# Five block-product passes, a seeded second DFT and ScalarE statistics in an FNet layer with a gated feed-forward

## The chip, the core and the metric

The kernel runs on one core of one Trainium2 chip. The metric is the device time of one execution in microseconds (us); less is better. Times given for a version are medians of several executions; beside them stands one execution that the hardware profiler recorded. The engines are PE (TensorE, matrix products into PSUM), DVE (VectorE), ACT (ScalarE), POOL (GpSimd) and SP (SyncE, whose queue here issues the DMA transfers). Each engine works through its own list of instructions in order, and waits on semaphores for the others.

## The reference

The input x has 2048 rows (the sequence) of 448 columns. A Fourier layer and a gated feed-forward layer follow each other, each on a normalised input and with a residual.

```python
a = jnp.einsum("bsd,ed->bse", x, dft_hid_re)
b = jnp.einsum("bsd,ed->bse", x, dft_hid_im)
y = jnp.einsum("ts,bse->bte", dft_seq_re, a) - jnp.einsum("ts,bse->bte", dft_seq_im, b)
...
g = jnp.einsum("bsd,df->bsf", x, w_gate)
u = jnp.einsum("bsd,df->bsf", x, w_up)
h = _gelu(g) * u
return jnp.einsum("bsf,fd->bsd", h, w_down)
...
h = x + _A_ref(_layernorm(x, axis=-1), A_dft_seq_re, A_dft_seq_im, A_dft_hid_re, A_dft_hid_im)
h2 = h + _B_ref(_layernorm(h, axis=-1), B_w_gate, B_w_up, B_w_down)
```

## The kernel before, in words

Every product is made with operands split into two float16 parts (a high and a low part), three matmuls for one. ACT writes the high part (`hi_part`, L107), DVE the low part from the difference (`lo_part`, L110).

**The sequence DFT** comes first and runs in 64 steps (`N_STEPS`, loop at L816). The first 16 steps make two of the eight pairs of row blocks at once. From step 16 on, four steps are a pass: a pair p (2 to 7) and one of its two parts, real or imaginary. A plain step reads one tile of the DFT matrix (wr, loaded by `seq_load`), splits it into ws (`seq_hi`, `seq_lo`, three steps ahead of its use) and multiplies it with the normalised x (xs): 24 matmuls of 448 columns. The last three passes (steps from `FAST` = 52 on) are made by Strassen-like block products: seven products of half-size blocks in place of eight, 42 matmuls of 224 columns in a step. They need sums of blocks of the DFT matrix (`fast_sums` on DVE, then `fast_raw` and `fast_split` for the two tiles of a unit), sums of blocks of x (the tiles t, `t_load` to `t_lo`), and at the end of the pass the seven products are put together on DVE (`fast_out`, e). A unit is listed two steps ahead of its use; in the last step of a pass its parts stand between the parts of `fast_out`. Both kinds of pass write zs, from which `z_turn` makes z by transposing DMAs.

**The second DFT** (`hid_mm`, L708) multiplies z of a pair p, in two halves g of 128 rows, with the hidden DFT matrix wh: 21 matmuls of 448 columns into a PSUM bank y. It stands on PE between the two halves of the sequence steps m and m + 1, with m = 19, 24, 29, 36, 44, 52, 60 for p = 0 to 6; p = 7 comes within the next stage. DVE then adds x to it (`hid_add`, L722; the tile hx, loaded one step before), takes the statistics of h (`ffn_moments`) and `rstd` makes the factor of the second normalisation.

**The order** is written by hand: the tables `early` (work listed at the start of a step, behind the step's own splits) and `after` (behind its first or second half of matmuls) say at which step a piece of work stands. Each engine's list follows from the order of these calls. Buffers rotate: six ws tiles, five wr tiles, seven PSUM banks for the passes and one bank, tr, for y.

**The feed-forward** follows: 42 gate and up products in three blocks of rows (`GateUp`), then the down products. Its weights are split by `Weights`, ten chunks f during the DFT (`DFT_F`) and four during the first block (`JIT_F`), stored to w_dram and read back as gw; the last three of the DFT stay in their three tiles.

Of the kernel before, what the change touches and what calls it, by code (L numbers as in the profile page):

```python
# [21 lines left out]
NB = 4  # L22
# [10 lines left out]
def kernel(  # L33
# [92 lines left out]
    def root(mv, tag):  # L126
        n = mv.shape[1]
        sd = small.tile([P, n], F32, tag=f"sd{n}", name=f"sd_{tag}")
        A.activation(sd, mv[:, :, 1], AF.Sqrt, scale=1.0 / X_SC**2, bias=eps_t)
        return sd  # L130
# [5 lines left out]
    def rstd(mv, sd, tag, pool=small):  # L136
# [4 lines left out]
        V.tensor_scalar(r[:, 1], mv[:, :, 1], EPS, -0.5 / X_SC**2, op0=ALU.add, op1=ALU.mult)  # L141
# [26 lines left out]
    def pair_tile(name):  # L168
        return ring.tile([P, 2, D], F32, tag="xh", bufs=5, name=name)

    def w_tile(name):
        return ring.tile([P, 28 * P], F16, tag="w", bufs=3, name=name)
# [25 lines left out]
    def ffn_rstd(q, j):  # L198
        tag = f"h{q}_{j}"
        mv = moments[q, j]  # L200
        moments[q, j] = mv, rstd(mv, root(mv, tag), tag, const)

    def ffn_stats(q, j, h):
        for g in range(2):
            ffn_moments(q, j, h, g)
        ffn_rstd(q, j)
# [18 lines left out]
    def ffn_norm(q, j, h):  # L225
        tag = f"h{q}_{j}"
        mv, r = moments.pop((q, j))
        xn = fops.tile([P, 2, D], F32, tag="xn", name=f"xn_{tag}")
        for g in range(2):
            normed(xn[:, g, :], h[:, g, :], mv, r, g)  # L230
        ffn[q, j] = xn

    def ffn_bias(q, j):
        mv, r = moments[q, j]
        V.scalar_tensor_tensor(mv[:, :, 1], mv[:, :, 0], -1.0, r, op0=ALU.mult, op1=ALU.mult)
# [81 lines left out]
    class Weights:  # L317


        def __init__(self, f):  # L320
            self.f = f
# [26 lines left out]
        def hi(self, of_raw):  # L348
            if of_raw:
                self.w = w_tile(f"gu_w{self.f}")  # L350
            for s0, s1, src in self.parts(of_raw):
                hi_part(self.slots(0, s0, s1, src), src, W_SC)
# [100 lines left out]
    FAST = N_STEPS - 12  # L453
    A_RAW = ("A12", "A11", "A22")
    FORMS = ("S1", "S2", "S3", "S4")
# [11 lines left out]
    def fast_sums(n):  # L467
        fast_s[n] = dft.tile([P, 8 * P], F32, tag="wr", bufs=5, name=f"sums{n}")
        fast_w[n] = [fast_tile(n, k, **place) for k, place in enumerate(fast_places(n))]
        raw, s, src, dst = fast_views(n)  # L470
        V.tensor_add(s[:, 0], raw[:, :, 3], raw[:, :, 2])
        V.tensor_sub(s[:, 1], s[:, 0], raw[:, :, 1])
        V.tensor_sub(s[:, 2], raw[:, :, 1], raw[:, :, 3])
        V.tensor_sub(s[:, 3], raw[:, :, 0], s[:, 1])
# [54 lines left out]
    def fast_halves(n, g):  # L529
        p, part, qq = step_of(n)  # L530
        hi, lo = [zs[p][:, g, l, part * D : (part + 1) * D] for l in range(2)]
        src = fast_e[n][:, g * D : (g + 1) * D]
        hi_part(hi, src)
        lo_part(lo, src, hi)

    def fast_out(n, k):
# [10 lines left out]
        def plus(dst, m, src):  # L547
            V.scalar_tensor_tensor(c[dst], fast_sum(n, m), sc, c[src], op0=ALU.mult, op1=ALU.add)
# [37 lines left out]
    def t_tile(j):  # L586

        if j in (0, 1):
            if j == 0:
                fast_t["01"] = fops.tile([P, 8 * D], F16, tag="xs", name="t01")  # L590
            return fast_t["01"][:, j * 4 * D : (j + 1) * 4 * D]
# [4 lines left out]
        if j == 6:  # L596
            return ring.tile([P, 4 * D], F16, tag="xh", bufs=5, name="t6")
        if j == 7:
            return prep.tile([P, 4 * D], F16, tag="raw", bufs=2, name="t7")
        return fops.tile([P, 4 * D], F16, tag="xn" if j == 2 else "tt", name=f"t{j}")  # L600
# [101 lines left out]
    def h_tile(q, j):  # L702
        hp[q, j] = pair_tile(f"hx{q}_{j}")
# [26 lines left out]
    gu = {}  # L730
    DFT_F = ((13, 17), (12, 20), (11, 25), (9, 29), (7, 33), (5, 37), (3, 41), (0, 45), (1, 48), (2, 50))
    JIT_F = range(4, 11, 2)
# [10 lines left out]
    for f, n in DFT_F:  # L743
        at(after, (n - 4, 0), lambda f=f: gu.update({f: Weights(f)}))
# [5 lines left out]

    turns = [(16, 0), (20, 1), (25, 1), (32, 0), (40, 0), (48, 0), (57, 0)]
    for p, (n, half) in enumerate(turns):
        b, j = divmod(p, 2)
        m = (19, 24, 29, 36, 44, 52, 60)[p]
        at(early, m - 1, lambda b=b, j=j: h_tile(b, j))
        for g in range(2):

            at(after, (m + g, int(p == 6 and g)), lambda p=p, g=g: hid_mm(p, g), lambda p=p, g=g: hid_add(p, g))
        at(after, (n, half), lambda p=p: z_turn(p))
        at(early, m + 2 if p < 5 else N_STEPS - 7 + p, lambda b=b, j=j: ffn_stats(b, j, hp[b, j]))  # L760
        at(after, (m + 2, 0), lambda b=b, j=j: h_store(b, j))
        if b < 2:

            m += 2 if p == 3 else 0
            at(early, m + 2, lambda b=b, j=j: ffn_norm(b, j, hp[b, j]))
# [7 lines left out]
    for j, n in ((4, 28), (5, 31), (6, 39), (2, 43), (3, 45), (0, 47), (1, 49), (7, 53)):  # L773
# [139 lines left out]
    gu[JIT_F[0]] = Weights(JIT_F[0])  # L913
    z_turn(NP - 1)
    down_sums(0)
    gu[JIT_F[1]] = Weights(JIT_F[1])
# [7 lines left out]
    gw = {f: gu[f].w for f in range(3)}  # L924

# [101 lines left out]
    class GateUp:  # L1027
# [7 lines left out]
        def bank(self, k):  # L1035
            pool, tag = ps_gu, "XYZ"[k]
            if self.block == 0 and self.t % 2 == 0:
                pool, tag = ps_dn, f"a{k}"
            if self.block > 0 and k == 1 and self.t % 2 == 0:
                pool, tag = ps_tr, "tr"  # L1040
            return pool.tile([P, 512], F32, tag=tag, name=f"p{'XYZ'[k]}_{self.name}")[:, : self.n]
# [74 lines left out]
    def gw_load(t):  # L1116
        gw[t] = w_tile(f"gw{t}")
# [74 lines left out]
    def dn_banks(p):  # L1192

        if p == 6:
            places = [(ps_gu, "X"), (ps_tr, "tr"), (ps_gu, "Z"), (ps_gu, "Y")]
        else:
            places = [(ps_dn, f"a{k}") for k in range(4)]
        acc_d[p] = [pool.tile([P, 512], F32, tag=tag, name=f"acc_d{p}_{k}") for k, (pool, tag) in enumerate(places)]
# [22 lines left out]
    def hr_load(p):  # L1221
        hr[p] = pair_tile(f"hr{p}")
# [45 lines left out]
    ps_gu = ctx.enter_context(tc.tile_pool(name="ps_gu", bufs=1, space=bass.MemoryType.PSUM, reuse_waits="tile"))  # L1268
    ps_dn = ctx.enter_context(tc.tile_pool(name="ps_dn", bufs=1, space=bass.MemoryType.PSUM, reuse_waits="tile"))
# [9 lines left out]
    for t in range(NF):  # L1279
# [77 lines left out]
        if w and w.f + 4 in JIT_F:  # L1357
            gu[w.f + 4] = Weights(w.f + 4)
# [181 lines left out]
```

## Time and profile before

| what | us |
|---|---|
| median of 3 executions (lowest to highest) | 710.85 (710.21 to 710.87) |
| the profiled execution | 711.16 |
| its span, first to last instruction | 708.7 |
| DVE busy in the span | 531.7 |
| ACT busy in the span | 353.3 |
| POOL busy in the span | 92.6 |

The profile names each instruction by its line in the source; a matmul's row shows out<-in by the program's names. Three views are used below: the page (shares, slices and the chain of work that ended last), the same chain in order of time (a start, a duration, what ran), and the timeline of one engine (a start, a duration, line and operation, how many, and in brackets the idle time before it with what ended it). "x2" means two instructions in a row. A lookup of short stretches gives each engine's busy time, the count of its instructions in parentheses, and the granted clock of PE.

### The profile page before, as it was taken

To read this page: it belongs to the slowest core of one execution; us is meant where nothing else is said; L and a number is where in the kernel's file an instruction comes from. 1 tells how busy PE (TensorE), PEld (TensorE's weight loads), DVE (VectorE), ACT (ScalarE), POOL (GpSimd) and SP (SyncE) were. 2 spreads that over 40 slices of the span, in tenths; PEclk is the share of its full clock that TensorE was granted. 3 is DMA by queue.
4 is the path that set the end of the run, shared out by engine and by line. 5 is a ranking of instruction groups with operands and counts; after the bars stand their busy time and mean duration, and the time that the engine had idled before them with its cause. 6 is when DMAs were issued, how large, how long until landed. Compare 5 with 4: busy or idle time off the path is not lost.

```text
span 708.7 us, 13039 instructions
## 1 busy us (share of the span) xinstructions
PE 702.7 (99%) x4952; PEld 480.3 (68%) x4952; DVE 531.7 (75%) x1176; ACT 353.3 (50%) x656; POOL 92.6 (13%) x88
## 2 busy tenths in 40 slices
PE   9999999999999999999999999999999999999998
PEld 5555555555555555798744444469999989999997
DVE  7997647486848779999647788557777867799885
ACT  5776523162516454544436566545556444565531
POOL 0000000000000000000133333311010110252224
PEclk9999999999999999999999999999999999999999
DMA  8797538999988969653655866796797977787612
GB/s 272 252 260 257 129 122 232 236 320 249 219 290 234 270 216 240 238 140 115 166 187 176 279 228 180 209 310 234 215 283 263 291 220 276 264 289 283 221 54 79
DMA packets 116030, 159.41 MB, mean 225 GB/s; under 512 B 61952, under 2 KB 80512, under 8 KB 115968
## 3 DMA queue, kind: packets, MB, share of 16 engines
q1 hardware_dynamic: 115968, 158.60, 73.6%
q8 instruction: 38, 0.62, 0.4%
q14 instruction: 24, 0.20, 0.1%
HBM read 110.33 MB, written 34.34 MB: 204 GB/s over the span
## 4 chain that ended last, share of the span: by engine, by line
PE 97%; DMA 1%; DVE 1%; SPq 0%; ACT 0%; issue 0%; POOL 0%; DVEq 0%; POOLq 0%; ACTq 0%
PE acc L648 33%; PE acc_d L1212 15%; PE pY L1010 14%; PE pZ L1010 9%; PE y L714 9%; PE pX L1010 9%; PE acc_f L520 7%; DMA hid_dram<-hs 1%; PE pw L102 1%; DVE hr L1476 0%; DVE hr L944 0%; DVE dn_s L1175 0%; DVE dn_s L1174 0%; DVE hr L972 0%; ACT u L1066 0%
## 5 line engine op out<-in xcount | busy, mean ns | idle before, releaser
L648 PE MATMUL acc<-xs,ws 128*128 128x448 f16 x1248 | 237.9, 352 | 0.0
L648 PEld LDWEIGHTS <-ws 128*128 128x128 f16 x1248 | 122.0, 98 | 113.9 <-DVE ws L114 0.2
L1010 PEld LDWEIGHTS <-gw 128*128 128x128 f16 x1365 | 133.4, 98 | 42.9
L1212 PE MATMUL acc_d<-wd,dn_w 128*128 128x224 f16 x1008 | 110.8, 259 | 1.2 <-ACT v L940 0.7
L1212 PEld LDWEIGHTS <-dn_w 128*128 128x128 f16 x1008 | 96.8, 98 | 3.6 <-issue 0.9
L1104 POOL TENSOR_TENSOR hs<-hs,c 128x256 f32<-128x256 f32 (+1 forms) x42 | 58.7, 1398 | 251.1 <-ACT c L1102 183.9
L1010 PE MATMUL pY<-hops,gw 128*128 128x256 f16 (+1 forms) x595 | 89.9, 294 | 0.0
L114 DVE SCALAR_TENSOR_TENSOR ws<-wr,ws 128x1024 f16<-128x1024 f32 (+2 forms) x66 | 75.1, 1140 | 9.5 <-ACT ws L108 7.8
L108 ACT ACTIVATE ws<-wr 128x1024 f16<-128x1024 f32 (+2 forms) x66 | 63.9, 982 | 21.2 <-DMA wr<-in_w_seq_dram 19.3
L714 PE MATMUL y<-wh,z 128*128 128x448 f16 x336 | 66.2, 352 | 0.0
L1010 PE MATMUL pZ<-hops,gw 128*128 128x256 f16 (+1 forms) x385 | 61.7, 294 | 0.0
L1010 PE MATMUL pX<-hops,gw 128*128 128x256 f16 (+1 forms) x385 | 61.7, 294 | 0.0
L220 POOL TENSOR_TENSOR wd_s<-wd 128x448 f32<-128x448 f32 x7 | 9.5, 1353 | 342.7 <-DVE r_h L142 341.9
L714 PEld LDWEIGHTS <-z 128*128 128x128 f16 x336 | 32.9, 98 | 30.1
L1055 ACT ACTIVATE pY<-pX 128x256 f32<-128x256 f32 (+1 forms) x42 | 18.4, 439 | 61.7 <-PE pX L1010 61.3
L520 PEld LDWEIGHTS <-ws 128*128 128x128 f16 x504 | 48.3, 98 | 0.9
L1010 PEld LDWEIGHTS <-gu_w 128*128 128x128 f16 x273 | 26.6, 98 | 31.9 <-issue 0.3
L1020 DVE SCALAR_TENSOR_TENSOR c<-pZ,u 128x256 f32<-128x256 f32 (+1 forms) x42 | 21.4, 511 | 33.0 <-PE pZ L1010 21.0
L1066 ACT ACTIVATE u<-pY 128x256 f32<-128x256 f32 (+1 forms) x42 | 19.1, 455 | 53.2 <-PE pY L1010 53.1
L112 DVE TENSOR_TENSOR dn_w<-dn_s,dn_w 128x640 f16<-128x640 f32 x48 | 41.1, 857 | 2.0 <-ACT dn_w L108 1.9
L108 ACT ACTIVATE dn_w<-dn_s 128x640 f16<-128x640 f32 x48 | 35.0, 730 | 12.7 <-DVE dn_s L1176 12.7
L1174 DVE TENSOR_TENSOR dn_s<-hid 128x256 f32<-128x256 f32 x54 | 25.4, 471 | 15.7 <-DMA hid<-hid_dram 15.6
(139 smaller groups left out, 868.8 us busy)
## 6 DMA issues: line engine op xcount, KB each, us to landing
gw<-w_dram SPq DMA_DIRECT2D x35, 896.0 KB, 5.9
wr<-in_w_seq_dram SPq DMA_DIRECT2D x100, 256.0 KB, 4.5
hid_dram<-hs SPq DMA_DIRECT2D x27, 512.0 KB, 6.5
hid<-hid_dram SPq DMA_DIRECT2D x54, 256.0 KB, 6.2
w_dram<-gu_w SPq DMA_DIRECT2D x14, 896.0 KB, 5.1
gu_raw<-in_w_gu_dram SPq DMA_DIRECT2D x28, 384.0 KB, 6.0
wr<-in_w_seq_dram SPq DMA_DIRECT2D x14, 512.0 KB, 5.9
x<-in_x_dram SPq DMA_DIRECT2D x16, 224.0 KB, 3.9
```

The lines of the kernel that those rows point to most:

```text
L108: A.activation(dst, src, AF.Copy, scale=scale)
L112: V.tensor_sub(dst, src, hi)
L114: V.scalar_tensor_tensor(dst, src, scale, hi, op0=ALU.mult, op1=ALU.subtract)
L520: PE.matmul(fast_sum(n, k), fast_a(n, i, lw, a), fast_b(j, lx, b), start=j == 0 and m == 0 and k % 2 == 0, stop=j == NT // 2 - 1 and m == ...
L648: PE.matmul(acc[key][:, :D], w[:, lw, block * P : (block + 1) * P], xs[c][:, lx, :], start=c == 0 and m == 0, stop=c == NT - 1 and m == 2,)
L714: PE.matmul(y[:, :D], z[p][:, lz, k, g * P : (g + 1) * P], wh[:, lw, k, :], start=k == 0 and m == 0, stop=k == 6 and m == 2,)
L1010: PE.matmul(ps, w[:, wl, wa + ws, :], ops[:, m + ms, :], start=first and n == 0, stop=last and n == len(terms) - 1, skip_group_check=True,)
L1020: V.scalar_tensor_tensor(dst, ps, SC, other, op0=ALU.mult, op1=ALU.add)
L1066: A.activation(self.u2, self.Y, AF.Copy, scale=SC)
L1104: G.tensor_mul(c22, c22, self.cols(self.c12))
L1174: V.tensor_add(s[:, 0:2], t[:, 0:2], t[:, 2:4])
L1212: PE.matmul(ps, w[:, la, a, :], wd[n][:, lb, b, :], start=n == 0 and m == 0 and opens, stop=n == NC - 1 and m == 2, skip_group_check=True,)
```

## The change

- `FAST` is 44 instead of 52: the passes of steps 44 to 51 are block products too, five passes in all. The block sums are made with three DVE instructions instead of four, with other signs, which `fast_out` and `fast_halves` undo.
- Second DFT, p = 0 to 6: ACT first copies x, scaled, into the bank y (`hid_seed`); the matmuls add to it (start is false). ACT then reads h out of the bank with its sum (`hid_out`), and squares it with the sum of squares. DVE's add and statistics fall away. p = 7 is as before.
- The normalisation of h for the first rows is made by ACT (`ffn_norm_act`) instead of DVE.
- `DFT_F` has nine chunks, earlier than before; chunk 12 moves to `JIT_F`. Chunks 0, 1 and 2 are stored and read back (`gw_first`) like the others.
- The tiles t are made at other steps, in other buffers; rings of tiles have fixed places; the PSUM banks of the feed-forward are taken in another order.

```diff
-    FAST = N_STEPS - 12
+    FAST = N_STEPS - 20
...
-        V.tensor_add(s[:, 0], raw[:, :, 3], raw[:, :, 2])
-        V.tensor_sub(s[:, 1], s[:, 0], raw[:, :, 1])
-        V.tensor_sub(s[:, 2], raw[:, :, 1], raw[:, :, 3])
-        V.tensor_sub(s[:, 3], raw[:, :, 0], s[:, 1])
+        by_block = raw.rearrange("p i b t -> p b i t")
+        V.tensor_add(s[:, 0:2], by_block[:, 1:3], by_block[:, 3:4].to_broadcast([P, 2, 2, P]))
+        V.tensor_add(s[:, 2], s[:, 1], raw[:, :, 1])
+        V.tensor_add(s[:, 3], raw[:, :, 0], s[:, 2])
...
+            s = -sc if m in (2, 4, 6) else sc
+            V.scalar_tensor_tensor(c[dst], fast_sum(n, m), s, c[src], op0=ALU.mult, op1=ALU.add)
...
+    def hid_seed(p, g):
+
+        y = ys[p, g] = ps_tr.tile([P, 512], F32, tag="tr", name=f"y_{p}_{g}")
+        A.activation(y[:, :D], hp[p // 2, p % 2][:, g, :], AF.Copy, scale=D_SC)
+
+    def hid_out(p, g):
+
+        q, j = divmod(p, 2)
+        if g == 0:
+            moments[q, j] = const.tile([P, 2, 2], F32, tag=f"mv_h{q}_{j}", name=f"mv_h{q}_{j}")
+        y, h, mv = ys[p, g][:, :D], hp[q, j][:, g, :], moments[q, j]
+        A.activation(h, y, AF.Copy, scale=1.0 / D_SC, accum_out=mv[:, g, 0:1])
+        A.activation(mv[:, g, 0:1], mv[:, g, 0:1], AF.Copy, scale=-1.0 / D)
+        A.activation(y, y, AF.Square, scale=1.0 / D_SC, bias=mv[:, g, 0:1], accum_out=mv[:, g, 1:2])
+
     def hid_mm(p, g):
 
-        pool, tag = (ps_dn, "a3") if p == NP - 1 and g else (ps_tr, "tr")
-        y = ys[p, g] = pool.tile([P, 512], F32, tag=tag, name=f"y_{p}_{g}")
+        if p == NP - 1:
+            ys[p, g] = bank_tile("a3" if g else "tr", f"y_{p}_{g}")
+        y = ys[p, g]
...
-                    start=k == 0 and m == 0,
+                    start=p == NP - 1 and k == 0 and m == 0,
                     stop=k == 6 and m == 2,
+                    skip_group_check=True,
...
-    DFT_F = ((13, 17), (12, 20), (11, 25), (9, 29), (7, 33), (5, 37), (3, 41), (0, 45), (1, 48), (2, 50))
-    JIT_F = range(4, 11, 2)
+    DFT_F = ((13, 17), (11, 20), (9, 22), (7, 25), (5, 27), (3, 30), (0, 32), (1, 35), (2, 37))
+    JIT_F = range(4, 13, 2)
...
+    for f, n in ((0, N_STEPS - 7), (2, N_STEPS - 4), (1, N_STEPS - 3)):
+        at(after, (n, 1), lambda f=f: gw_first(f))
...
         at(early, m - 1, lambda b=b, j=j: h_tile(b, j))
+        at(early, m, lambda p=p: hid_seed(p, 0))
         for g in range(2):
 
-            at(after, (m + g, int(p == 6 and g)), lambda p=p, g=g: hid_mm(p, g), lambda p=p, g=g: hid_add(p, g))
+            at(after, (m + g, int(p == 6 and g)), lambda p=p, g=g: hid_mm(p, g), lambda p=p, g=g: hid_out(p, g))
+            if g == 0:
+                at(after, (m, 0), lambda p=p: hid_seed(p, 1))
...
-    for j, n in ((4, 28), (5, 31), (6, 39), (2, 43), (3, 45), (0, 47), (1, 49), (7, 53)):
+    for j, n in ((0, 17), (1, 20), (4, 24), (5, 29), (6, 36), (2, 39), (3, 42), (7, 45)):
         at(after, (n - 2, 1), lambda j=j: t_load(j))
```

What stands on the engines at the places that matter, first ACT around step 60 (pair 6). Before, with ws62 and ws63 the units of steps 62 and 63, e59 and zs7 the results of the pass that ends with step 59:

```order
L551 ACTIVATE e59_3382<-acc_f56_0_3184 128x224
L108 ACTIVATE ws61_0_3362<-wr61_3255 128x768
L108 ACTIVATE ws61_1_3363<-sums61_3361 128x1024
L108 ACTIVATE zs7_3383<-e59_3382 128x448 x2
L108 ACTIVATE ws62_0_3438<-wr62_3316 128x768
L108 ACTIVATE ws62_1_3439<-sums62_3437 128x1024
L108 ACTIVATE ws63_0_3514<-wr63_3404 128x768
L108 ACTIVATE ws63_1_3515<-sums63_3513 128x1024
```

With the change (y_6_0 and y_6_1 are the banks of the two halves of pair 6, hx3_0 its x and then its h, mv its sums):

```order
L540 ACTIVATE e59_3588<-acc_f56_0_3392 128x224
L108 ACTIVATE ws61_0_3569<-wr61_3461 128x768
L108 ACTIVATE ws61_1_3570<-sums61_3568 128x1024
L108 ACTIVATE zs7_3589<-e59_3588 128x448 x2
L108 ACTIVATE ws62_0_3644<-wr62_3523 128x768
L108 ACTIVATE ws62_1_3645<-sums62_3643 128x1024
L699 ACTIVATE y_6_0_3653<-hx3_0_3574 128x448
L707 ACTIVATE hx3_0_3574,mv_h3_0_3697<-y_6_0_3653 128x448
L708 ACTIVATE mv_h3_0_3697<-mv_h3_0_3697 128x1
L709 ACTIVATE y_6_0_3653,mv_h3_0_3697<-y_6_0_3653,mv_h3_0_3697 128x448
L699 ACTIVATE y_6_1_3701<-hx3_0_3574 128x448
L108 ACTIVATE ws63_0_3727<-wr63_3610 128x768
```

Five ACT instructions for y stand between the splits of units 62 and 63; the first of them is ahead of the second DFT of pair 6 on PE, which stays in the middle of step 60. Around step 52 the list of pair 5 reads the same, with units 54 and 55.

Second, DVE at the same place, from the end of the pass's results. Before:

```order
L112 TENSOR_TENSOR zs7_3383<-e59_3382,zs7_3383 128x448 x2
L471 TENSOR_TENSOR sums62_3437<-wr62_3316 128x256
L472 TENSOR_TENSOR sums62_3437<-sums62_3437,wr62_3316 128x256
L473 TENSOR_TENSOR sums62_3437<-wr62_3316 128x256
L474 TENSOR_TENSOR sums62_3437<-wr62_3316,sums62_3437 128x256
L114 SCALAR_TENSOR_TENSOR ws62_0_3438<-wr62_3316,ws62_0_3438 128x768
L114 SCALAR_TENSOR_TENSOR ws62_1_3439<-sums62_3437,ws62_1_3439 128x1024
L724 SCALAR_TENSOR_TENSOR hx3_0_3368<-y_6_0_3469,hx3_0_3368 128x448
```

With the change:

```order
L112 TENSOR_TENSOR zs7_3589<-e59_3588,zs7_3589 128x448
L114 SCALAR_TENSOR_TENSOR zs7_3589<-e59_3588,zs7_3589 128x448
L460 TENSOR_TENSOR sums62_3643<-wr62_3523 128x512
L461 TENSOR_TENSOR sums62_3643<-sums62_3643,wr62_3523 128x256
L462 TENSOR_TENSOR sums62_3643<-wr62_3523,sums62_3643 128x256
L114 SCALAR_TENSOR_TENSOR ws62_0_3644<-wr62_3523,ws62_0_3644 128x768
L114 SCALAR_TENSOR_TENSOR ws62_1_3645<-sums62_3643,ws62_1_3645 128x1024
```

The sums are three instructions, each on the result of the one before, and the add of x is gone; the place of the sums behind the zs of the pass is the same.

Third, ACT at the end of step 23 and in step 24 (pair 1). Before, where only splits of coming units follow the zs of the pass:

```order
L108 ACTIVATE zs2_1134<-acc2_10_1174 128x448
L108 ACTIVATE zs2_1134<-acc2_11_1175 128x448
L108 ACTIVATE ws27_1391<-wr27_1297 128x1024
L108 ACTIVATE ws28_1446<-wr28_1338 128x1024
L108 ACTIVATE ws29_1514<-wr29_1388 128x1024
```

With the change (gu_w9 is weight chunk 9, y_1_0 and hx0_1 belong to pair 1):

```order
L108 ACTIVATE zs2_1158<-acc2_10_1202 128x448
L108 ACTIVATE zs2_1158<-acc2_11_1203 128x448
L108 ACTIVATE ws27_1441<-wr27_1330 128x1024
L108 ACTIVATE gu_w9_1386<-gu_s9_1340 128x512 x2
L699 ACTIVATE y_1_0_1448<-hx0_1_1402 128x448
```

The seed of pair 1 stands behind the zs of step 23, one split and two weight instructions; PE's second DFT of pair 1 stays in the middle of step 24.

More of the change, by code (lines that the diff above doesn't have):

```diff
@@ L200, in ffn_rstd @@
         mv = moments[q, j]
[L201 to L206, printed above, removed]
+        moments[q, j] = mv, rstd(mv, root(mv, tag, D), tag, const, D)
     wd32, wd_s = {}, {}
@@ L1194, in dn_banks @@
         if p == 6:
-            places = [(ps_gu, "X"), (ps_tr, "tr"), (ps_gu, "Z"), (ps_gu, "Y")]
+            places = ("X", "tr", "Z", "Y")
         else:
-            places = [(ps_dn, f"a{k}") for k in range(4)]
-        acc_d[p] = [pool.tile([P, 512], F32, tag=tag, name=f"acc_d{p}_{k}") for k, (pool, tag) in enumerate(places)]
+            places = ("a0", "a1", "a2", "a3")
+        acc_d[p] = [bank_tile(tag, f"acc_d{p}_{k}") for k, tag in enumerate(places)]
         sums = [(acc_d[p][k // 2], k % 2) for k in range(7)]
```

101 lines of the change are left out of this document (50 added, 51 removed).

## The prediction

> **What bounds the kernel now.** The page first, for the engines' shares and the chain that ended last:
>
> ```profile
> span 708.7 us, 13039 instructions
> PE 702.7 (99%) x4952; PEld 480.3 (68%) x4952; DVE 531.7 (75%) x1176; ACT 353.3 (50%) x656; POOL 92.6 (13%) x88
> DVE  7997647486848779999647788557777867799885
> PE 97%; DMA 1%; DVE 1%; SPq 0%; ACT 0%; issue 0%; POOL 0%; DVEq 0%; POOLq 0%; ACTq 0%
> ```
>
> PE is busy 99% and is 97% of the chain: a matmul removed is time gained, and a wait put in front of PE is time lost. The DVE line matters second: slices 15 to 18 (266 to 337 us) show nines, just where the three seven-product passes run. The same chain in order of time tells where PE stands and what one matmul costs:
>
> ```profile
> 106.92 18.16 PE acc L648 x96
> ...
> 125.08 3.97 PE y L714 x21
> ...
> 155.73 3.97 PE y L714 x21
> ...
> 195.45 3.97 PE y L714 x21
> ...
> 239.72 3.97 PE y L714 x21
> ...
> 295.69 28.18 PE acc_f L520 x294
> 323.87 3.97 PE y L714 x21
> 327.84 6.04 PE acc_f L520 x63
> ```
>
> A plain pass of four steps is 96 matmuls of 448 columns, 18.16 us, 4.54 a step. A product pass is 168 matmuls of 224 columns at 28.18 / 294 = 0.0959 us: 16.10 us, 4.02 a step. The y rows are the second DFT, 21 matmuls between the halves of a step, and PE never waits for them. From these rows each step's start on PE follows: step 60's first half (21 matmuls, 2.01 us) ends at 323.87, so step 60 begins at 321.86, and step 56 168 matmuls earlier, at 305.75.
>
> Third, the timeline of DVE around step 60, and of ACT there:
>
> ```profile
> 309.36 0.42 DVE L471 TENSOR_TENSOR sums<-wr 128x256 f32<-128x256 f32 x1
> ...
> 320.99 0.42 DVE L471 TENSOR_TENSOR sums<-wr 128x256 f32<-128x256 f32 x1
> ...
> 324.35 1.22 DVE L114 SCALAR_TENSOR_TENSOR ws<-sums,ws 128x1024 f16<-128x1024 f32 x1
> 325.48 1.41 DVE L548 SCALAR_TENSOR_TENSOR e<-acc_f,e 128x224 f32<-128x224 f32 x4
> 326.93 1.22 DVE L112 TENSOR_TENSOR zs<-e,zs 128x448 f16<-128x448 f32 x2
> 328.07 0.42 DVE L471 TENSOR_TENSOR sums<-wr 128x256 f32<-128x256 f32 x1
> ...
> 329.54 0.95 DVE L114 SCALAR_TENSOR_TENSOR ws<-wr,ws 128x768 f16<-128x768 f32 x1
> 330.80 1.23 DVE L114 SCALAR_TENSOR_TENSOR ws<-sums,ws 128x1024 f16<-128x1024 f32 x1 [0.31 <-ACT ws L108]
> ```
>
> ```profile
> 326.32 1.17 ACT L108 ACTIVATE zs<-e 128x448 f16<-128x448 f32 x2 [2.69 <-DVE e L548]
> 327.40 0.83 ACT L108 ACTIVATE ws<-wr 128x768 f16<-128x768 f32 x1
> 329.71 1.06 ACT L108 ACTIVATE ws<-sums 128x1024 f16<-128x1024 f32 x1 [1.48 <-DVE sums L474]
> 330.68 0.83 ACT L108 ACTIVATE ws<-wr 128x768 f16<-128x768 f32 x1
> ```
>
> The three L471 rows are the starts of units 58, 61 and 62 on DVE (59 and 60 lie between the first two). Three units take 11.63 us, 3.88 each; the one that shares its step with the pass's results takes 320.99 to 328.07, 7.08. So DVE needs 18.7 us for a pass for which PE needs 16.1, and it falls back: unit 58 begins 3.6 us after step 56 began on PE, unit 62 begins 6.2 us after step 60 did. It costs nothing, since a unit is used two steps after the step in which it is listed: unit 60's halves are ready just as step 60 starts. PE recovers no lead; the y matmuls give DVE the time back.
>
> **The change part by part. (1) Two more product passes.** Steps 44 to 51 drop 192 matmuls of 448 columns and gain 336 of 224: 2 x (18.16 - 16.10) = 4.1 us off PE. Nothing hides this, it is on the chain.
>
> **(2) The seed.** Until now PE needed nothing of ACT for y. Now hid_mm (p = 0 to 6) adds to a bank that ACT must have filled, and the seed stands in ACT's queue behind all that the step lists before it. Place by place, I ask when ACT reaches the seed against when PE reaches the y matmuls. One seed of 448 columns I price by this zs row, 0.54 us; half or half as much again would shift each place by 0.3.
>
> *p = 6, step 60.* The list shows seed y_6_0 right behind the second half of unit 62's split. The trace has that very instruction: 329.71 + 1.06 = 330.77. Seed to 331.31, signal to PE about 0.1: 331.4. PE is there at 323.87. It waits 7.6 us. ACT cannot come sooner, because that split waits for the sums of unit 62, these stand on DVE behind the zs halves of the pass just ended, and those need PE's last products of step 59. Idle ACT time does not help.
>
> *p = 5, step 52.* The same list one pass pair earlier: unit 54 behind the results of pass 48 to 51, which has no y in it, as 56 to 59 has none. If DVE begins unit 50 3.6 us behind, as unit 58 above, the wait is again 7.6. The 7.6 us PE loses at step 52 does not carry over: two rings of buffers (six ws tiles, three units) stop DVE and ACT from running further ahead, and at the end of pass 52 to 55 DVE must again wait for PE's results. So both places pay, 15.2 together. Bounds for one: with no backlog at all DVE still needs, after PE's last product, the last e (about 0.4), the zs halves (326.89 to 328.07, 1.2), sums to split (328.07 to 330.77, 2.7), the seed 0.6, 5.0 in all against 2.0 on PE: 3.0 at least. From above: two us more backlog and dearer sums (below): 10. I take 7.6, read straight from the rows.
>
> *p = 1 to 4, in plain steps and at step 44.* Here the seed follows the zs copies, which wait for the end of the step before. Rows for what lies between:
>
> ```profile
> 122.85 0.54 ACT L108 ACTIVATE zs<-acc 128x448 f16<-128x448 f32 x1 [1.67 <-PE acc L648]
> 123.29 1.99 ACT L108 ACTIVATE ws<-wr 128x1024 f16<-128x1024 f32 x2
> ...
> 148.95 0.54 ACT L108 ACTIVATE zs<-acc 128x448 f16<-128x448 f32 x1 [1.68 <-PE acc L648]
> ...
> 150.34 0.82 ACT L108 ACTIVATE xs<-xn_h 128x256 f16<-128x256 f32 x2
> 151.06 1.09 ACT L108 ACTIVATE xs<-tt 128x768 f16<-128x768 f32 x2
> ...
> 157.90 0.92 ACT L108 ACTIVATE gu_w<-gu_raw 128x512 f16<-128x512 f32 x2
> ...
> 159.67 1.14 ACT L108 ACTIVATE gu_w<-gu_s 128x512 f16<-128x512 f32 x2
> ```
>
> p = 1: zs to 123.29 (the next starts there), ws27 1.0, gu_w9 1.1, seed 0.54, signal: 126.0 against 125.08, 0.9 us. p = 3: after the end of step 35 (195.45 - 2.27 = 193.18) zs 0.5, ws39 1.0, gu_w1 0.9, seed and signal 0.6: 196.2 against 195.45, 0.8. p = 2: from 148.95, zs, ws31, gu_w5, the four xs, ws32, gu_w5, seed: 6.8 us against 155.73 - 148.95 = 6.8, nothing. p = 4: zs and the four xs, seed: 2.8 against 2.0, and the tt these wait for is late on a full DVE: 1.1. p = 0: nothing, ACT has time to spare before y (idle for 4.97 us in the row of 94.52 below). Together 2.8, from 0 (ACT quicker) to 8 (the x tile for the seed lands late each time):
>
> ```profile
> 94.52 0.54 ACT L108 ACTIVATE zs<-acc 128x448 f16<-128x448 f32 x1 [4.97 <-issue]
> ...
> 118.19 0.51 SPq L704 DMA_DIRECT2D hx<-in_x_dram  x1
> hx<-in_x_dram SPq DMA_DIRECT2D x8, 448.0 KB, 6.2
> ```
>
> For p = 1 that is 118.2 + 0.5 + 6.2 = 124.9, just in time, with more loads ahead of it in the queue now.
>
> **(3) The clock after a long hold.** In the quoted windows (the last columns before DMA are the granted clock) it is lost soon after PE stops: the last matmuls start at 703.92, and from 707.90 it is 0.53. At the start the 48 transposes go 13 and 17 per us:
>
> ```profile
> 703.92 0.59 PE acc_d L1212 x6
> 707.90:708.70 0.80, 0.00 (x0) 0.00 (x0) 0.00 (x0) 0.00 (x0) 0.00 (x0) 0.53 0.00 0
> 2.40:3.40 1.00, 1.00 (x13) 1.00 (x11) 1.00 0.56 191
> 4.40:5.40 1.00, 1.00 (x17) 1.00 (x15) 1.00 1.09 344
> ```
>
> So 3.4 us without matmuls halve the clock and some 3 us of work bring it back. A hold of 7.6 us pays it: from 0 to 3.97 (all 21 y at half speed) each; I take half of 3.4, 1.7, twice: 3.4. The short holds of (2) are too short for it. The Trainium skill ("TensorE: Matmul & The Clock Gate", Part 1) has a free-running window of about 3.4 us both for losing the clock and for winning it back; by that rule a restart costs 1.7 to 3.4, and the span would lie up to 3.4 above mine.
>
> **(4) What costs nothing.** h's sums and squares (three ACT instructions in place of one DVE add and four statistics) wait for PE and are waited for by nothing soon: the seed of the second half comes some 2 us later, and PE needs it 4 us after. The DVE time this frees lies outside the units above. Sums in three instructions: 128x512 is not in the trace; between 0.42 (one of 256 columns) and 0.84 (two), by the way from 0.42 to the 0.95 of 768 columns 0.69; but each now waits for the one before, so a unit stays near 3.9. At 0.84 it is 0.6 more per pass, in the upper bound. Reloading three gw tiles lies in slices where PE has two to three steps in hand; the fifth chunk in the gate and up stage adds to ACT and DVE what each of the four adds there now, and PE shows no wait in that stage; uncovered it would be well under 2 us. t tiles earlier fill DVE in steps 39 to 43, which is in p = 4.
>
> **Sum:** 708.7 - 4.1 + 2.8 + 15.2 + 3.4 = 726.0 for the span. The profiled execution took 711.16, 2.46 outside its span, and lies 0.31 above the median: 726.0 + 2.15 = 728.2.
>
> **The rivals.** *(B) Faster:* ACT reaches each seed in time and only (1) counts: 708.7 - 4.1 + 2.15 = 706.7. For it: ACT is busy 50%, and DVE sheds 14 adds and 28 statistics. It decides from the point where unit 62's sums begin 7.6 us sooner, 1.3 us before step 60; against it, they need results of step 59. *(C) The short chain:* DVE keeps no backlog, so the two holds are 3.0 each, and too short to lose the clock: 708.7 - 4.1 + 2.8 + 6.0 + 2.15 = 715.5. For it: DVE does less; against: 18.7 against 16.1 per pass is untouched by what it sheds. *(D) More holds:* weight chunks packed into steps 13 to 41 crowd the DMA queue, the x tiles come late and the short holds become 8; sums cost 0.84 and the long ones 9 each, restarts 3 each: 708.7 - 4.1 + 8 + 18 + 6 + 2.15 = 738.8.
>
> **How the numbers follow.** Forecast 0.73, B 0.07, C 0.08, D 0.12. Time 728.2. The range leaves out B, part of C and the outer half of D: 716.0 to 737.0. About 0.2% (1.4 us) is what a measurement tells from no change; only something between B and C could land there: faster 0.07, same 0.02, slower 0.91.
>
> **What would show it.** In the profile after, PE's idle time before y must be put down to ACT y (the seed): about 7 us twice, near steps 52 and 60, and about 1 us at three earlier places; the granted clock must dip right behind the two long ones; acc_f must count 840 matmuls and acc 1056; DVE's unit spacing must stay near 3.9 and 7.1. The forecast is wrong if PE shows no gap before y, if unit 54 or 62 begins within 3 us of step 52 or 60, or if the gaps stand before acc_f instead.

## The result, and the profile after

The changed kernel takes 750.98 us (median of 4 executions, 749.39 to 752.52), the kernel before 710.56 on the same chip: a ratio of 1.0569, 95% interval 1.0543 to 1.0595. The forecast was 728.2 with 716 to 737: slower was right, but the loss is 40 us where 17 were forecast. The profiled execution took 751.84 with a span of 750.0, so 41.3 us of span are to be explained (750.0 - 708.7).

The page of the changed kernel, the lines that answer to those shown of before:

```profile
span 750.0 us, 13440 instructions
...
PE 711.8 (95%) x5096; PEld 496.8 (66%) x5096; DVE 534.2 (71%) x1164; ACT 392.9 (52%) x758; POOL 87.5 (12%) x88
...
PE   9999998989789899598799999999999999999998
...
PEclk9999999999989899799799999999999999999999
...
PE 74%; DVE 9%; DMA 6%; ACT 4%; SPq 3%; issue 3%; POOL 0%; ACTq 0%; DVEq 0%; POOLq 0%
```

The PE line has holes where it had none, all in the first half of the span, the sequence DFT, and the granted clock dips in slices beside them. The chain of work is no longer PE alone (97%): DVE, DMA and ACT stand in it. The view of PE's waits (us in total, times, longest) says what PE waited for:

```profile
PE y L718 <- ACT y L699: 30.9, 6, 8.6
...
PE acc_d L1225 <- DVE dn_w L112: 1.3, 1, 1.3
...
PE acc_f L508 <- DVE ws L114: 0.2, 1, 0.2
```

L699 is the seed. Six waits, 30.9 us. PE's timeline has them one by one, p = 1 to 6 below, behind one undisturbed block (start, duration, how many, and in brackets the wait ahead of it):

```profile
102.86 4.14 PE L718 MATMUL y<-wh,z 128*128 128x448 f16 x21
...
127.62 5.82 PE L718 MATMUL y<-wh,z 128*128 128x448 f16 x21 [2.46 <-ACT y L699]
...
162.23 4.13 PE L718 MATMUL y<-wh,z 128*128 128x448 f16 x21 [2.12 <-ACT y L699]
...
208.73 6.28 PE L718 MATMUL y<-wh,z 128*128 128x448 f16 x21 [6.62 <-ACT y L699]
...
258.49 6.99 PE L718 MATMUL y<-wh,z 128*128 128x448 f16 x21 [3.44 <-ACT y L699]
...
310.67 6.51 PE L718 MATMUL y<-wh,z 128*128 128x448 f16 x21 [8.62 <-ACT y L699]
...
361.01 6.93 PE L718 MATMUL y<-wh,z 128*128 128x448 f16 x21 [7.66 <-ACT y L699]
```

Two losses stand in each row. The bracket is the wait. The duration is the second: 21 matmuls take 4.13 undisturbed, and 5.82 to 6.99 behind five of the six waits, 11.9 us more in all. The clock in the stretch of a wait and in the block behind it, p = 1, 2 and 4 (the columns are the stretch, its length, busy time of PE, PEld, DVE, ACT and POOL with counts, granted clock, DMA share, GB/s):

```profile
125.17:127.62 2.45, 0.00 (x1) 0.00 (x1) 2.45 (x7) 0.97 (x3) 0.00 (x0) 1.00 1.07 431
127.62:133.43 5.81, 5.81 (x22) 2.64 (x22) 3.24 (x7) 1.27 (x2) 0.00 (x0) 0.71 1.09 323
160.11:162.23 2.12, 0.00 (x1) 0.00 (x1) 2.12 (x7) 0.60 (x2) 0.00 (x0) 1.00 1.03 425
162.23:166.36 4.13, 4.13 (x22) 2.14 (x22) 2.65 (x6) 1.28 (x2) 0.00 (x0) 1.00 1.20 350
255.04:258.49 3.45, 0.01 (x2) 0.00 (x1) 3.42 (x11) 2.48 (x6) 0.00 (x0) 0.85 0.50 152
258.49:265.48 6.99, 6.99 (x23) 3.03 (x23) 3.24 (x9) 0.00 (x0) 0.00 (x0) 0.58 0.39 75
```

A wait of 2.45 us lost the clock, one of 2.12 did not; the last section shows what decides between them. The account: the first matmul of the next stage starts at 385.87 after and 345.76 before, 40.1 later. Of that 30.9 are the waits, 11.9 the slow blocks, about 1.0 a rest of 0.16 at each wait (from the second block of a pair to the next wait PE takes 0.16 more than in an undisturbed run), 0.2 the wait before acc_f; less 4.1 for the two product passes: 39.9. The feed-forward adds 1.2.

What made the seed late differs by place. ACT's timeline, first p = 1 and p = 3, then p = 5:

```profile
127.02 0.55 ACT L699 ACTIVATE y<-hx 128x448 f32<-128x448 f32 x1 [1.48 <-DMA hx<-in_x_dram]
...
208.13 0.55 ACT L699 ACTIVATE y<-hx 128x448 f32<-128x448 f32 x1 [5.92 <-DMA hx<-in_x_dram]
...
309.13 1.06 ACT L108 ACTIVATE ws<-sums 128x1024 f16<-128x1024 f32 x1 [1.54 <-DVE sums L462]
310.09 0.53 ACT L699 ACTIVATE y<-hx 128x448 f32<-128x448 f32 x1
```

At p = 1 to 3 the seed waits for its x tile (1.55 us of it at p = 2, not shown). SP's queue shows why at p = 3: the load is issued at 202.07, behind two groups of transposing DMAs whose issue takes 7.21 and 5.00 us. The row by itself is the same load before:

```profile
182.60 7.21 SPq L657 DMA_TRANSPOSE z<-zs  x4
...
194.96 5.00 SPq L294 DMA_TRANSPOSE hops<-xs  x2
...
202.07 0.42 SPq L692 DMA_DIRECT2D hx<-in_x_dram  x1
```

```profile
191.18 0.44 SPq L704 DMA_DIRECT2D hx<-in_x_dram  x1
```

Of the 10.9 us between the two, 6.8 are only the waits of p = 1 and 2 and the slow block behind the first, which put everything on PE later. Against PE's arrival at the block the load is 4.1 us later: 0.04 us ahead of it now (202.11), 4.1 ahead before (195.29). At p = 1 and 2 the lead fell from 6.7 and 7.6 us to 4.4 and 5.3. Since such a load takes 6.2 us to land (the median of both kernels), the old lead at p = 3 would have been too short as well, by an estimated 2 us; before, nobody felt it, because DVE needed the tile only behind the block.

At p = 4, 5 and 6 ACT itself comes late, at 5 and 6 behind the split of weight sums as the forecast had it. DVE's sums of three units, the last of them unit 54, first instruction of each:

```profile
296.37 0.68 DVE L460 TENSOR_TENSOR sums<-wr 128x512 f32<-128x512 f32 x1
...
300.29 0.69 DVE L460 TENSOR_TENSOR sums<-wr 128x512 f32<-128x512 f32 x1
...
307.43 0.69 DVE L460 TENSOR_TENSOR sums<-wr 128x512 f32<-128x512 f32 x1
```

The spacing is 3.92 and 7.14, and the unit in front of the seed begins at 307.43, 5.4 us after PE came to the y block (302.05).

### The profile page after: what moved, and what is told of

Read it like the earlier page. It is cut to its first block, busy times and chain, and to the rows that moved or that the text cites. A ratio compares the mean times of both kernels' runs of the same rounds, so it can differ in the third digit from the quotient of the medians.

```text
span 750.0 us, 13440 instructions
## 1 busy us (share of the span) xinstructions
PE 711.8 (95%) x5096; PEld 496.8 (66%) x5096; DVE 534.2 (71%) x1164; ACT 392.9 (52%) x758; POOL 87.5 (12%) x88
## 4 chain that ended last, share of the span: by engine, by line
PE 74%; DVE 9%; DMA 6%; ACT 4%; SPq 3%; issue 3%; POOL 0%; ACTq 0%; DVEq 0%; POOLq 0%
PE acc L636 17%; PE acc_d L1225 14%; PE pY L1023 12%; PE y L718 10%; PE pZ L1023 8%; PE pX L1023 8%; PE acc_f L508 4%; DMA hx<-in_x_dram 3%; ACT ws L108 2%; DMA gu_raw<-in_w_gu_dram 2%; SPq L657 1%; DVE ws L114 1%; DVE sums L460 1%; DMA hid_dram<-hs 1%; DVE e L537 1%
## 5 line engine op out<-in xcount | busy, mean ns | idle before, releaser
L636 PE MATMUL acc<-xs,ws 128*128 128x448 f16 x1056 | 201.2, 352 | 0.0
L1023 PEld LDWEIGHTS <-gw 128*128 128x128 f16 x1443 | 140.9, 98 | 51.6
L636 PEld LDWEIGHTS <-ws 128*128 128x128 f16 x1056 | 103.2, 98 | 96.4 <-DVE ws L114 0.2
L718 PE MATMUL y<-wh,z 128*128 128x448 f16 x336 | 78.0, 396 | 30.9 <-ACT y L699 30.9
L1023 PE MATMUL pY<-hops,gw 128*128 128x256 f16 (+1 forms) x629 | 98.0, 298 | 0.0
L508 PEld LDWEIGHTS <-ws 128*128 128x128 f16 x840 | 80.4, 98 | 1.8 <-DVE ws L114 0.5
L1023 PE MATMUL pZ<-hops,gw 128*128 128x256 f16 (+1 forms) x407 | 67.1, 298 | 0.0
L1023 PE MATMUL pX<-hops,gw 128*128 128x256 f16 (+1 forms) x407 | 67.1, 298 | 0.0
L508 PE MATMUL acc_f<-t,ws 128*128 128x224 f16 x480 | 57.1, 259 | 0.2 <-DVE ws L114 0.2
L508 PE MATMUL acc_f<-xs,ws 128*128 128x224 f16 x360 | 45.6, 259 | 0.0
L707 ACT ACTIVATE hx<-y 128x448 f32<-128x448 f32 x14 | 7.6, 543 | 65.7 <-PE y L718 65.7
```

The costliest lines, as they stand in the source:

```text
L508: PE.matmul(fast_sum(n, k), fast_a(n, i, lw, a), fast_b(j, lx, b), start=j == 0 and m == 0 and k % 2 == 0, stop=j == NT // 2 - 1 and m == ...
L636: PE.matmul(acc[key][:, :D], w[:, lw, block * P : (block + 1) * P], xs[c][:, lx, :], start=c == 0 and m == 0, stop=c == NT - 1 and m == 2,)
L718: PE.matmul(y[:, :D], z[p][:, lz, k, g * P : (g + 1) * P], wh[:, lw, k, :], start=p == NP - 1 and k == 0 and m == 0, stop=k == 6 and m == ...
L1023: PE.matmul(ps, w[:, wl, wa + ws, :], ops[:, m + ms, :], start=first and n == 0, stop=last and n == len(terms) - 1, skip_group_check=True,)
```

## Experiments

Nine kernels. Every ratio is to the kernel before, run beside it on the same chip (medians 711.0, 710.98 and 710.79 us).

### The seed two steps earlier, the x tile three

```diff
-        at(early, m - 1, lambda b=b, j=j: h_tile(b, j))
-        at(early, m, lambda p=p: hid_seed(p, 0))
+        at(early, m - 4, lambda b=b, j=j: h_tile(b, j))
+        at(early, m - 2, lambda p=p: hid_seed(p, 0))
```

> The changed kernel with one thing moved: each seed of a first half is listed two steps earlier, and the x tile's load three steps earlier; all else stays. Theory (the loss is the seed's place in ScalarE's queue): the trace of the changed kernel has 30.9 us of PE waiting for the seed and y blocks that are 12.8 us longer than undisturbed ones behind those waits; both go, and only the two more product passes are left: 751 - 30.9 - 12.8 = 707, within 2 us, no wait of PE before y, the clock at 1.00 through the y blocks. Rival one (the seed is only the last in a row that is late anyway): the waits move to the next thing that ScalarE makes (acc_f behind ws, or acc behind zs), 720 or more. Rival two (the clock falls for another cause than the waits, say the power of product passes): the waits go but the y blocks stay above 6 us, 720.

Measured: 711.86 us, ratio 1.0004 (0.9992 to 1.0016). All six waits and every slow block are gone, 39 us with two lines moved. One new wait stands in PE's list, before the second block of p = 5:

```profile
PE y L718 <- ACT y L699: 2.3, 1, 2.3
```

```profile
288.24 1.06 ACT L108 ACTIVATE ws<-sums 128x1024 f16<-128x1024 f32 x1 [1.54 <-DVE sums L462]
289.20 0.53 ACT L707 ACTIVATE hx<-y 128x448 f32<-128x448 f32 x1
```

These two rows of ACT's timeline show its cause: y's first block was done by 285.1, but ACT empties the bank only at 289.20, behind the split of sums, and the second seed needs the bank. It is the change's long wait again, at another door. The theory stands; its number (707) was 5 too low: 2.3 is this wait, 1.1 a later start of the matmul stream (the first y block at 95.43, in the changed kernel at 94.35; the other runs have 94.39 to 95.35), and the remaining 1.2 is the spread between executions (the spans of the two profiled ones are 40.3 us apart, the medians 39.1).

### Only the x tile earlier

```diff
-        at(early, m - 1, lambda b=b, j=j: h_tile(b, j))
+        at(early, m - 4, lambda b=b, j=j: h_tile(b, j))
```

> The changed kernel with only the x tile's load listed three steps earlier; the seeds stay where the change put them. Theory (in plain steps it is the x tile's transfer that is late, in the product steps the order on ScalarE): the waits before y of p = 1, 2 and 3, now 2.46, 2.12 and 6.62 us, fall to what the order on ScalarE alone gives, 0.9, 0 and 0.8, and the y blocks of p = 1 and 3 come back to about 4 us; p = 4, 5 and 6 stay (3.4, 8.6, 7.7). Saved: 9.5 of waits and 4.2 of slow matmuls, so 737. Rival (the transfer's lateness only covers ScalarE's own): the three waits shrink by less than half, and the time stays above 745.

Measured: 740.05 us, ratio 1.0411 (1.0385 to 1.0437), 11 less than the changed kernel. PE's y blocks of p = 1, 2 and 3:

```profile
127.83 4.13 PE L718 MATMUL y<-wh,z 128*128 128x448 f16 x21 [1.96 <-ACT y L699]
...
160.24 4.13 PE L718 MATMUL y<-wh,z 128*128 128x448 f16 x21 [1.60 <-ACT y L699]
...
201.78 4.13 PE L718 MATMUL y<-wh,z 128*128 128x448 f16 x21 [1.66 <-ACT y L699]
```

p = 4 to 6 wait 3.44, 8.63 and 7.67 as in the changed kernel. So the late x tile was the larger part of p = 3's 6.62, but the seed still comes late by 1.6 to 2.0 at each plain step, where 0.9, 0 and 0.8 were expected. ACT's timeline shows that at all three places a split ahead of the seed waits in its turn for a transfer, of a tile of the DFT matrix:

```profile
125.25 1.06 ACT L108 ACTIVATE ws<-wr 128x1024 f16<-128x1024 f32 x1 [0.98 <-DMA wr<-in_w_seq_dram]
...
157.66 1.06 ACT L108 ACTIVATE ws<-wr 128x1024 f16<-128x1024 f32 x1 [1.68 <-DMA wr<-in_w_seq_dram]
...
199.41 1.06 ACT L108 ACTIVATE ws<-wr 128x1024 f16<-128x1024 f32 x1 [0.98 <-DMA wr<-in_w_seq_dram]
```

From each of these splits to the seed ACT works without a gap. Without their waits the seed would be late by about 1.0, 0 and 0.7: ACT's order by itself costs what was expected, and the rest is the DMA queue. No run separates what made the queue later (more weight chunks, x loads for the tiles t at other steps, longer transposes).

### Three product passes instead of five

```diff
-    FAST = N_STEPS - 20
+    FAST = N_STEPS - 12
```

> The changed kernel with three product passes as before and everything else of the change kept, seeds included. Theory (a long wait stands where a unit of weight sums is in work at the step of the seed): p = 5 at step 52 meets no sums any more, so its wait falls from 8.6 to 1 to 3.5 us; p = 6 at step 60 stays near 7.7; p = 1 to 4 stay. PE gets 4.1 us more of plain matmuls, loses 5 to 7.5 of waiting and up to 2.5 of slow matmuls: 745 to 748. Rival (the waits are due to the seed alone, in whatever pass): p = 5 stays above 7 and the time is about 755.

Measured: 736.74 us, ratio 1.0363 (1.0346 to 1.038). The blocks of p = 5 and p = 6:

```profile
300.62 4.14 PE L718 MATMUL y<-wh,z 128*128 128x448 f16 x21
...
348.60 5.93 PE L718 MATMUL y<-wh,z 128*128 128x448 f16 x21 [7.67 <-ACT y L699]
```

p = 5 does not wait at all, p = 6 waits as long as ever. The mechanism is as expected, a unit of sums in work at the step of the seed makes the long wait; the size was missed by 8 us and more, since p = 5 lost its whole 8.6 and its slow block, p = 4 fell from 3.44 to 1.44 and its slow block went too. p = 4 thus belongs with them: in the changed kernel unit 46 is listed in step 43, its split stands ahead of the zs copies on ACT, which begin at 254.31, 1.3 after step 44 began on PE (255.04 - 2.01), and its sums keep DVE from the tt that the seed's forerunners need.

### No seed: VectorE adds x and takes the statistics

`hid_out` is `hid_add` again, the matmuls start the bank, and `ffn_rstd` is preceded by `ffn_moments` on DVE, as before the change; five passes and the nine chunks stay.

```diff
-        at(early, m, lambda p=p: hid_seed(p, 0))
...
-                    start=p == NP - 1 and k == 0 and m == 0,
+                    start=k == 0 and m == 0,
```

> The changed kernel without the seed and without ScalarE's statistics: x is added by VectorE behind the second DFT and h's statistics are taken by VectorE, as before the change; the five product passes and the nine chunks in the DFT stay. Theory (the loss hangs on the seed alone): no wait of PE before y, the y blocks at about 4 us, and the two more product passes give what their matmuls cost: 707 to 708. Rival (with five product passes VectorE, which now also adds and takes statistics, falls behind, and the seed only showed it): PE waits before acc_f or acc for ws or zs, 712 to 725.

Measured: 712.08 us, ratio 1.0019 (1.0003 to 1.0035). The loss hangs on the seed (this run leaves out ScalarE's statistics too, but the run above with early seeds kept them and lost the waits as well); yet the 4.1 us of the passes do not show, because DVE now holds the one bank in the same way:

```profile
PE y L719 <- DVE hx L730: 3.2, 2, 2.0
```

```profile
291.83 5.81 PE L719 MATMUL y<-wh,z 128*128 128x448 f16 x21 [1.99 <-DVE hx L730]
```

PE waits twice (1.23 and 1.99) for the add that empties the bank between the two halves, and one of these waits lost the clock: 3.2 + 1.7. The rival was right that DVE is too full for this, but the wait stands before y, not before acc_f (0.5).

### Matmuls on zeros in the place of the waits

This run tests the clock alone: the waits stay, but PE is kept at work in them. Zero weights add nothing to the running sum they are put on.

```diff
+    FILL = {24: 24, 36: 66, 44: 34, 52: 88, 60: 78}
+
+    def hid_fill(n):
+        to = fast_sum(n, 0) if n >= FAST else acc[(*step_of(n)[:2], 0)][:, :HD]
+        for _ in range(FILL[n]):
+            PE.matmul(to, zero, wh[:, 0, 0, 0:HD], start=False, stop=False, skip_group_check=True)
...
+        if m in FILL:
+            at(after, (m, 0), lambda n=m: hid_fill(n))
```

> The changed kernel with matmuls on a tile of zeros put in front of the first y block of p = 1, 3, 4, 5 and 6, as many as fill the waits seen there (24, 66, 34, 88 and 78 of 224 columns, 0.096 us each: 2.3, 6.3, 3.3, 8.4 and 7.5 us); they add zero to a running sum. The seed and all that it waits for stay. Theory (a wait costs its length and besides that some 2.5 us of slow matmuls, because PE stood idle): the waits before y shrink to a rest under 1 us each, every y block takes 4.1 us, the granted clock stays at 1.00, and the time is 12 less than the 751 of the changed kernel, 739. Rival (the slow y blocks have another cause, such as the seed's bank or the z tiles): the y blocks stay at 5.8 to 7.0 us and the time at 751.

Measured: 742.8 us, ratio 1.0444 (1.0429 to 1.0459), 8 less than the changed kernel though PE does 290 matmuls more. p = 2, which had no fillers, and p = 5 with them (the first row's bracket names a DMA that ended at that moment; ACT's timeline has the seed there waiting 2.74 for its x tile):

```profile
161.14 5.82 PE L728 MATMUL y<-wh,z 128*128 128x448 f16 x21 [2.69 <-DMA w_dram<-gu_w]
...
299.29 8.60 PE L709 MATMUL acc_f<-wh,zero 128*128 128x224 f16 x88
308.08 4.13 PE L728 MATMUL y<-wh,z 128*128 128x448 f16 x21 [0.20 <-ACT y L702]
```

All five filled places take 4.13 us for their block, with p = 3 still waiting 2.11. So the slow blocks come of PE's idleness and of nothing in y or z. That the time is not 739 lies in p = 2: its wait grew to 2.69 here and cost the clock, 2.3 in all over the changed kernel, and p = 3's wait grew by 2.0.

### The seed one step earlier

```diff
+        at(early, m - 4, lambda b=b, j=j: h_tile(b, j))
+        at(early, m - 1, lambda p=p: hid_seed(p, 0))
```

> The changed kernel with the first seeds listed one step earlier instead of two, and the x tiles three steps earlier. Theory (what the seed must not stand behind is the row of the step itself: in the product steps the halves of the pass just ended and the sums behind them): p = 6's seed then follows the split that ended at 324.0 in the run with early seeds, so it is there at 324.6 against 323.6, a wait of about 1 us in place of 7.7; p = 5 likewise 1; p = 1 to 4 none. In all 711.9 plus 2 to 3: 714 to 715. Rival (the seed is late by the whole lead of the sums, two steps): p = 5 and 6 still wait 4 us or more and lose the clock, 725.

Measured: 711.74 us, ratio 1.0008 (0.9999 to 1.0017). No first block waits at all, p = 5 and 6 included: the expectation had the seed one unit too far back. ACT's timeline shows it ahead of that step's e and of the split at 323.37:

```profile
320.47 0.53 ACT L699 ACTIVATE y<-hx 128x448 f32<-128x448 f32 x1
...
323.37 1.06 ACT L108 ACTIVATE ws<-sums 128x1024 f16<-128x1024 f32 x1 [1.37 <-DVE sums L462]
```

PE came to the block at 324.29, and the seed was done at 321.0, so one step of lead gives 3.3 us, and the whole loss of the long places lies in the row of the seed's own step. The second block of p = 5 waits 2.28 here as well, and this time it lost the clock (5.82 us for the block).

### Early only for p = 5 and 6

```diff
+        at(early, m - 4 if p > 4 else m - 1, lambda b=b, j=j: h_tile(b, j))
+        at(early, m - 2 if p > 4 else m, lambda p=p: hid_seed(p, 0))
```

> The changed kernel with the early place given only to the seeds of p = 5 and 6 (and their x tiles three steps earlier); p = 0 to 4 stay as changed. Theory (each place pays for itself): the waits of p = 1 to 4 stay (14.6 us, with 7.3 of slow matmuls behind them), those of p = 5 and 6 go (16.3 and 5.5), and the wait of 2.3 before the second y block of p = 5 comes: 751 - 21.8 + 2.3 = 731.5. Rival (the waits of p = 1 to 4 shift the work so that later ones cost nothing of their own): less than 15 us are saved, 736 or more.

Measured: 730.99 us, ratio 1.029 (1.0251 to 1.033), as the theory has it (731.5); with executions from 728.2 to 735.1, a match to half a microsecond is luck. The places pay each for themselves: p = 1 to 4 still wait 1.90, 2.14, 7.13 and 3.43.

### The second block of p = 5 half a step later

On top of the seeds two steps earlier:

```diff
-            at(after, (m + g, int(p == 6 and g)), lambda p=p, g=g: hid_mm(p, g), lambda p=p, g=g: hid_out(p, g))
+            at(after, (m + g, int(p >= 5 and g)), lambda p=p, g=g: hid_mm(p, g), lambda p=p, g=g: hid_out(p, g))
```

> The kernel with the early seeds (first seeds two steps, x tiles three steps earlier), and with the second y block of p = 5 put half a step later, as p = 6 has it. With the early seeds alone the time was 711.9 beside 711.0 of the kernel before, and PE still waited 2.28 us for the second seed of p = 5: ScalarE empties the first y block only behind a split of weight sums, and the one bank is seeded again after that. Theory (that wait is the last loss, and the two product passes then show in the time): the wait shrinks to 0.3 or less and the time falls by 2.0 to 2.3, to 709.5, 0.2% under the kernel before. Rival (PE arrives earlier at the next product step, whose sums are then late): PE waits 2 us before acc_f instead, and the time stays at 711.5 to 712.

Measured: 708.45 us, ratio 0.9961 (0.9947 to 0.9975). That is 2.5 us or 0.4% under the kernel before, with an interval that leaves out 1, and 42.5 under the changed one. The wait is down to what was expected, and no other wait of PE in the steps of the DFT is above 0.3 us:

```profile
PE y L718 <- ACT y L699: 0.3, 1, 0.3
```

### The same with three passes

```diff
-    FAST = N_STEPS - 20
+    FAST = N_STEPS - 12
```

> The fastest version so far (first seeds two steps and x tiles three steps earlier, the second y block of p = 5 half a step later) with three product passes in place of five. Theory (the two more passes are worth what their matmuls take, 2 x (18.16 - 16.10) = 4.1 us, and nothing else of the change is worth anything on PE's path): 708.45 + 4.1 = 712.5, with 1248 and 504 matmuls of the two kinds. Rival (part of the gain of the fastest version comes from ScalarE's statistics and the nine chunks in the DFT, which free VectorE): 710 to 711, as the kernel before or under it.

Measured: 711.24 us, ratio 1.0004 (0.9995 to 1.0013), with executions from 710.4 to 712.4. The forecast of 712.5 was 1.3 too high. Each against the kernel before beside it, five passes are worth 3.0 us over three (2.5 under it and 0.5 over it), less than the 4.1, and by the medians alone the rival is not excluded. The two profiled runs tell it sharper, from the first y block to the first matmul of the next stage, which leaves out how early the stream started. Five passes, then three:

```profile
94.41 4.13 PE L718 MATMUL y<-wh,z 128*128 128x448 f16 x21
...
342.62 1.46 PE L1023 MATMUL pX<-hops,gw 128*128 128x512 f16 x6
```

```profile
95.35 4.14 PE L718 MATMUL y<-wh,z 128*128 128x448 f16 x21
...
346.84 1.46 PE L1023 MATMUL pX<-hops,gw 128*128 128x512 f16 x6
```

248.2 against 251.5 us, 3.3 less; five passes have 0.8 us of small waits in that stretch (0.3, 0.3 and 0.2), three have none. 3.3 + 0.8 = 4.1: the matmuls are worth what their rows said. The kernel before takes 251.5 for this stretch too (345.76 - 94.27), so ScalarE's statistics and the nine chunks alone gain nothing on PE's path.

## Why the prediction was right, and where it was wrong

**(1) Two more product passes, 4.1: right**, measured as 4.1 in the last pair of runs. This was the change's whole gain, and it is in the 708.45. The counts are those forecast, 1056 matmuls of acc and 840 of acc_f.

**(2) p = 5 and 6, 15.2: right.** 8.62 and 7.66 against 7.6 each (7.5 by its own rows), in the row that was named, behind the split of the unit whose sums wait for the pass just ended; with no such unit (three passes) p = 5 waited for nothing.

**(2) p = 1 to 4, 2.8 with 0 to 8: wrong, it is 14.6.** This is the first step that failed. The prediction worked out ACT's list for all four, but looked at the x tile's load at p = 1 alone, where it came out "just in time". At p = 3 the load was issued only as PE came to the block, and even the bound for a late tile (8 for all four) was drawn too low. With the tile early the waits were still 1.96, 1.60 and 1.66, and there too the excess over the 0.9, 0 and 0.8 of the prediction's list is a transfer that came late (of wr). So at p = 1 to 3 ACT's order was read rightly; the step that failed is the DMA queue, which was taken to be in time. For p = 4 it left out the unit of sums listed in the step before, the very thing that it had found for p = 5 and 6: 3.44 in place of 1.1 (with three product passes 1.44).

**(3) The clock, 3.4: wrong, it is 11.9 and the rests of 0.16.** The second step that failed, in two ways. "The short holds of (2) are too short for it" fell with the first wait of 2.45 us, so that five places paid where two were counted; and each paid 1.7 to 2.9 where 1.7 was taken. With work in the place of the wait the blocks took 4.13 again, so it is the idleness that costs. The 3.4 us of idleness by which the prediction called them too short was a misreading of the trace before: 703.92 is the last piece of PE on the chain, not PE's last matmul. PE worked to 705.35 (the windows 704.00:706.00 and 705.25:705.50 have it busy for 1.35 and 0.10), and the clock fell at 707.95 (0.89 in 707.75:708.00, 1.00 up to there), after 2.6 us.

The Trainium skill ("TensorE: Matmul & The Clock Gate", Part 1) has the clock drop after an idle window of about 3.4 us, in windows that run free of the kernel. The traces agree on the windows: the half clock lasts 3.41, 6.83 or 10.24 us in the changed kernel, one, two or three times 3.41, and the five restarts cost 1.7 to 2.9, inside the 1.7 to 3.4 that the prediction worked out from it (1.45 is the least in any run). They do not agree that a whole window must be idle: stretches of 1.99 to 2.46 us lost the clock here, and the measurement decides.

**(4) What costs nothing: right.** DVE kept 3.92 and 7.14 for a unit, the new sum of 512 columns took 0.68 to 0.69 us where 0.69 was read off, and acc_f waited 0.2. Of the feed-forward's 1.2 us, 0.8 is a longer wait for a reload of the hidden tiles (dn_w, 1.3 us). That wait is 0.5 us in the kernel before and 0.2 to 2.0 in runs that share the whole feed-forward, and with three passes and the late seeds that stage takes 362.8 (735.3 - 372.46) as before (362.9, 708.7 - 345.76): so it varies from run to run. Whether the change has a share in it is open: the other runs with the seed have 363.0 to 364.9, and the kernel before has one trace.

**The rivals.** C had the long waits at 3.0 each; they are 8.62 and 7.66. D had the direction of the error (late x tiles, dearer restarts) and stopped at 738.8 because it kept two restarts of three us and 8 us of short waits. B is the kernel with the seeds early and the second block moved, 706.7 forecast against 708.45: the seed could be had for nothing, only not in the place that it was given.

## What to carry to other kernels

An instruction that the critical engine newly waits for must stand in its engine's list ahead of everything that itself waits for the same step; here one step of lead, with its operand's load three steps earlier, was worth 39 us, and the engine's idle time (ACT was busy 52%) said nothing of it. Follow the operand of such an instruction too, through the DMA queue, at each of its places and not at one. And price a wait of PE of two microseconds or more with the slow matmuls behind it: here they added some 40% to the waits' own length.

## What the hardware showed

The clock was kept over idle stretches of up to 1.96 us, and lost in every one from 2.69; in between, over all these runs, it went both ways (lost after 1.99, 2.03, 2.28 and 2.46, kept after 2.11, 2.12, 2.14, 2.28, 2.29 and 2.40). What decided is where the stretch lay. In each trace all changes of the granted clock lie on one grid of 3.41 us. Put on that grid, all 28 waits before y that are longer than 1.2 us fall in order: where PE was idle for 1.99 us or more within one cell, the clock fell to half at the end of the cell, and where the most was 1.98 us it did not. The two waits of 2.28 us show it. With seeds two steps earlier a cell ended within the wait, at 290.65; with seeds one step earlier the whole wait lay in one cell (the idle time is the length less the first busy time, the clock the third number from the end):

```profile
287.24:290.65 3.41, 1.92 (x21) 1.76 (x19) 3.04 (x5) 2.35 (x6) 0.00 (x0) 1.00 0.14 47
290.65:294.06 3.41, 2.62 (x14) 1.36 (x14) 3.12 (x5) 2.53 (x5) 0.00 (x0) 1.00 0.32 112
```

```profile
288.06:291.47 3.41, 1.13 (x8) 0.55 (x6) 2.94 (x5) 3.30 (x9) 0.00 (x0) 1.00 0.48 159
291.47:294.88 3.41, 3.41 (x11) 1.40 (x10) 3.22 (x5) 0.78 (x1) 0.00 (x0) 0.50 0.40 141
```

Idle for 1.49 and 0.79 us the clock stayed at 1.00; idle for 2.28 it was 0.50 for the next cell. Each loss made a block of 21 matmuls 1.45 to 2.9 us longer.

An ACT instruction with a sum beside its output leaves a second one in the trace, ACTIVATION_READ_ACCUMULATOR, 0.19 us each; there are 28 of them here, 5.4 us of ACT that the change's text does not show.
